# Output tiles kept in the weight buffers, stores behind the last load, and a new plan for a gated linear attention and spatial gating kernel

## The chip, the cores and the metric

The kernel runs on one core of one Trainium2 chip. The metric is the device time of one execution in microseconds, lower is better. The engines have short names: PE is the matrix engine, DVE the vector engine, ACT the scalar engine, POOL the GpSimd engine and SP the engine that issues nearly all transfers here. Each takes its instructions in the order in which the program gives them.

## The reference

Two layers follow each other. The first is a gated linear recurrence over 768 time steps for 4 batches and 8 heads of width 48; the second is a gated MLP that mixes over the sequence.

```python
# q, k, v, alpha: (B=4, H=8, S=768, D=48), float32
for t in range(S):
    state = alpha[:, :, t, :, None] * state + einsum('bhd,bhe->bhde', k[:, :, t], v[:, :, t])
    y[:, :, t] = einsum('bhd,bhde->bhe', q[:, :, t], state)
x = y.transpose(0, 2, 1, 3).reshape(B, S, H * D)          # (4, 768, 384)

h = maximum(x @ w_in, 0)                                   # w_in (384, 1024)
u, v = h[..., :512], h[..., 512:]
v_n = (v - mean(v)) / sqrt(var(v) + 1e-6)                  # over the last axis
v_s = einsum('ts,bsd->btd', w_spatial, v_n) + b_spatial[None, :, None]
out = (u * v_s) @ w_out                                    # (4, 768, 384), float32
```

## The kernel before, in words

The sequence is cut into 24 chunks of 128 rows, six for each of the four batches, numbered through. A chunk of the first layer loads four tiles, `ac` (alpha), `kc`, `qc` and `vc`, of 192 KB each. The first six chunks are loaded as three pairs of 384 KB. ACT takes the logarithm of `ac` into `la`. PE forms the running sum `cum` with a triangular matrix, and ACT takes exponentials of it: `binv`, the positive one in place, and `bc`, the decay of the whole chunk. POOL makes `kt` from `kc` and `binv`, DVE makes `qt` from `qc` and `cum`. PE transposes both into a PSUM bank (`pt`), and they are copied to `kqT`. PE then forms the scores, DVE masks them into `ptm` (two per chunk, called `m`), and PE adds the masked scores times the values `vb` and the queries times the carried state to `y`.

The state goes from chunk to chunk within a batch. PE forms its update `tp` (the operation `upd`), DVE adds it to the old state (`z`), `S` multiplies it by the decay (L334), and `sb` copies the two diagonal blocks to a bf16 tile `sbd` in two casts (L209). The next chunk's `y` reads `sbd`. `S` and `sb` may go to POOL or to DVE.

The output `y` is cast to `x_sb`, transposed on PE and copied to `xT`, which is the input of the second layer. There, for each batch, `v` (six tiles of 128x512) passes through ACT to `v_sb`. Its mean and variance come from DVE (`stats` and `mvs`) or, for the pairs of tiles that `ACT_STATS` names, from sums that ACT accumulates (L822 and L833) followed by three small DVE operations (`mv`). `rstd` is made on ACT and the normalised `vn` on DVE. `u` (eight groups of three matmuls) goes to `uT`. `s` (eight groups of six matmuls, `ps<-w_spT,vn`) is evacuated to `vsb` by DVE with the bias, and POOL multiplies it with `uT` to `gT`. The last `s` group takes its bias from a matmul and makes `gT` on DVE at once. `o` (six tiles per batch, four matmuls each) is evacuated by ACT and stored from SP.

The fp32 weights come in pieces of 768 KB into two buffers of the pool `raws` (`raw_w`) and are cast to bf16 tiles. The rows of `w_spatial` pass through three buffers `w_row` and are transposed into `w_spT`.

No order is written out by hand. Every operation is an `Op` with the engines that may run it, a planned duration, the operations that it waits for and a priority. `schedule` takes, again and again, the operation that can start first by these planned durations, and emits it; the instruction order on every queue comes from that. `PATIENCE` shifts the start that a kind of operation is compared by, `ENGINES` holds planned durations, `LD`, `LP`, `WT` and `ST` are those of transfers, and the argument `lat` is the time after which the result of an operation counts as there. `PIECES` places the weight loads among the others. While PE would be idle in the plan before 40 us, `schedule` puts matmuls of a tile `junk` in (L199), which compute nothing that is used and keep PE busy.

The output tiles go through a pool of four buffers `o_sb`, and their stores stand in SP's queue among the loads:

```python
def evac(eng, ps):
    hold["o"] = outp.tile([128, DM], FP32, name="o_sb")
    copy(eng, hold["o"], ps[:, 0:DM])
```

Of the kernel before, what the change touches and what calls it, by code (L numbers as in the profile page):

```python
# [9 lines left out]
FP32 = mybir.dt.float32  # L10
BF16 = mybir.dt.bfloat16
# [40 lines left out]
class Clock:  # L52
# [19 lines left out]
        return end  # L72


PATIENCE = {"ev": -0.3, "v": -0.1, "be": 0.2, "g": -0.3, "sb": -0.1, "bb": 0.3, "ln": 0.1, "z": -0.1, "S": 0.2, "o": -0.1, "cast": -0.2, "rs": 0.1}
ENGINES = {
    "kt": {"POOL": 0.87},
    "vb": {"POOL": 0.47},
    "S": {"POOL": 0.57, "DVE": 0.27},
    "sb": {"POOL": 0.79, "DVE": 0.36},  # L80
    "vn": {"DVE": 0.33},
    "xe": {"ACT": 0.38},
    "ev": {"DVE": 0.61, "ACT": 0.91},
    "u": {"ACT": 0.38, "DVE": 0.47},
    "o": {"ACT": 0.38},
}
PAIRS = (0, 1, 2)
ACT_STATS = ((0, 0), (3, 4), (2, 2), (3, 2))
PIECES = {
    "w_in": ((0, "vc", 0, 0.35), (0, "kc", 2, 0.15)),  # L90
    "w_sp": ((0, "vc", 4, 0.35), (0, "qc", 6, 0.25), (0, "qc", 6, 0.25)),
    "w_out": (0, "vc", 6, 0.35),
}


def schedule(ops, fill, warm_from, warm_to):

    free = {}
    clock = Clock()
    todo = list(ops)  # L100
    while todo:
        best = None
        for n, op in enumerate(todo):
            if any(d.end is None for d in op.deps):
                continue
            ready = max([d.end + d.lat for d in op.deps], default=0.0)
            waits = [slot.ring.free_at(k) for k, slot in enumerate(op.take)]
            if None in waits:
                continue
            ready = max([ready] + waits)  # L110
            for eng, dur in op.eng.items():
                start = max(ready, free.get(eng, 0.0))
                key = (round(start + (0.5 * dur if len(op.eng) > 1 else 0.0) + op.wait, 2),
                       ready if eng == "DMA" else op.prio)
                if best is None or key < best[0]:
                    best = (key, n, eng, start, dur)
        assert best is not None, "nothing can start"
        _, n, eng, start, dur = best
        op = todo.pop(n)
        if eng == "PE":  # L120
            if op.take and start < warm_to:
                t = max([free.get(eng, 0.0), warm_from] + [slot.ring.free_at(k) for k, slot in enumerate(op.take)])
                while True:
                    each = 0.00042 if clock.warm(t) else 0.00084
                    cols = min(192, int((start - t) / each) // 32 * 32)
                    if cols < 96:
                        break
                    fill.append(cols)
                    t = clock.run(t, 0.00042 * cols, cols)
            end = clock.run(start, dur, op.cols)  # L130
        else:
            end = start + dur
        for slot in op.take:
            slot.ring.taken.append(slot)
        free[eng] = end
        op.end = end
        op.emit(eng)
# [3 lines left out]
def kernel(  # L141
# [12 lines left out]
    nc = tc.nc  # L154

    B, H, S, D = q.shape
# [16 lines left out]
    IO = 3  # L173
    WK = 3
    NB, NKP = 3, 2
    LD, LP, WT, ST = 0.97, 1.46, 2.35, 0.8
    NRAW, NROW = 2, 3
    raws = ctx.enter_context(tc.tile_pool(name="raws", bufs=NRAW))
    io_pool = ctx.enter_context(tc.tile_pool(name="io", bufs=IO))
    work = ctx.enter_context(tc.tile_pool(name="work", bufs=WK))  # L180
# [13 lines left out]
    def bank(pool, shape, dtype, **kw):  # L194

        t = pool.tile(shape, dtype, **kw)
        flat = t if len(shape) == 2 else t.rearrange("p a b -> p (a b)")
        for cols in fill:
            nc.tensor.matmul(out=flat[:, 0:cols], lhsT=junk[:, 0:128], rhs=junk[:, 0:cols], start=True, stop=True)  # L199
        fill.clear()  # L200
        return t

# [15 lines left out]
    ut_ones = consts.tile([128, 128], BF16, name="ut_ones")  # L218
    ident = consts.tile([128, 128], BF16, name="ident")
    mask4 = consts.tile([128, 4, 128], BF16, name="mask4")  # L220
    junk = consts.tile([128, 192], BF16, name="junk")
    ones_row = consts.tile([1, 128], BF16, name="ones_row")
    ones_col = consts.tile([128, 1], BF16, name="ones_col")
    eps_tile = consts.tile([128, 1], FP32, name="eps_tile")
# [66 lines left out]
    def op(key, *args, **kw):  # L291

        users = kw.pop("use", ())
        o = Op(*args, **kw)
        for s in users:
            s.users.append(o)
        ops.append(o)
        made[key] = o
        o.wait = PATIENCE.get(key[0], 0.0)
        return o  # L300

    def got(*keys):
        return [made.get(x) for x in keys]
# [86 lines left out]
    def pair(j):  # L390
# [33 lines left out]
        for par in range(2):  # L424
# [42 lines left out]
                    out=ktp[:, par, :, :, 0:D].rearrange("p hp s d -> p (hp s) d"),  # L467
                    in0=st["kc"][:, :, par, :], in1=st[f"binv{par}"])

            op(("ktp", j, par), {"POOL": 0.87, "DVE": 0.47}, None, ktf, got(("einvp", j, par), ("kc", 2 * j)) + tr_users("k", jo), prio=P + 4)  # L470

            def qtf(_, par=par):
                nc.vector.tensor_mul(
# [116 lines left out]
    def first(i):  # L590
# [13 lines left out]

        j = i // 2
        jo = j - NKP
        dma(("ac", i), LD, load("ac", alpha), io_users("ln", j), P)
        dma(("kc", i), LD, load("kc", k), io_users("kt", j), P + 0.1)
        dma(("qc", i), LD, load("qc", q), io_users("qt", j), P + 0.2)
        dma(("vc", i), LD, load("vc", v), io_users("vb", j), P + 0.3)  # L610

        la, kt, qt = [x[j % NKP][:, i % 2].rearrange("p (hp s) d -> p hp s d", s=2) for x in (lap_bufs, ktp_bufs, qtp_bufs)]

# [196 lines left out]
    def second_v(b, tt):  # L810
# [33 lines left out]
        if on_act:  # L844
            def mv(_):
                d = bt[b]
                nc.vector.tensor_scalar_mul(out=d["mvs"][:, two, 0], in0=d["sums"][:, 0, two], scalar1=1.0 / DH)
                nc.vector.tensor_tensor(
                    out=d["mvs"][:, two, 1], in0=d["mvs"][:, two, 0], in1=d["mvs"][:, two, 0], op=ALU.mult)
                nc.vector.scalar_tensor_tensor(  # L850
                    out=d["mvs"][:, two, 1], in0=d["sums"][:, 1, two], scalar=1.0 / DH, in1=d["mvs"][:, two, 1],
                    op0=ALU.mult, op1=ALU.subtract)

            op(("mv", b, t0), "DVE", 0.4, mv, got(("bn", b, t0), ("bn", b, tt)), prio=6.0)

        def rs(_):
            d = bt[b]
# [38 lines left out]
    def second_s(b, dsl, th):  # L896
        last = b == B - 1 and dsl == NDS - 1 and th == 1
        mms = []
        if last:
            mms.append(mm(  # L900
                lambda ps: ps[:, 0:TH], lambda: ones_row, lambda: b_sp_sb[:, th * TH:(th + 1) * TH], True, False))
        for st in range(NT):
            mms.append(mm(
                lambda ps: ps[:, 0:TH], lambda st=st: bt[b]["vn"][:, st, dsl * 128:(dsl + 1) * 128],
                lambda st=st: w_spT[:, st, th * TH:(th + 1) * TH], st == 0 and not last, st == NT - 1))
        hold = {}
        cols = slice(th * TH, (th + 1) * TH)

        def evac(eng, ps):
            if last:  # L910
                nc.vector.tensor_tensor(
                    out=bt[b]["gT"][:, dsl, cols], in0=ps[:, 0:TH], in1=bt[b]["uT"][:, dsl, cols], op=ALU.mult)
            else:
                hold["vs"] = small.tile([128, TH], FP32, name="vsb", bufs=4)
                nc.vector.tensor_tensor(out=hold["vs"], in0=ps[:, 0:TH], in1=bsp_bc[:, th, :], op=ALU.add)  # L915

        Q = 1000.0 + 100 * b + 20 + th * NDS + dsl
        us = got(("u", b, dsl, th))
        pdeps = [[made[("vn", b, t)] for t in tt] for tt in ((0, 1, 2, 3), (4, 5))]
        us = us + got(*[("we", 3 * th + t) for t in range(3)])  # L920
        group(("s", b, dsl, th), mms, 0.165, [made[("v", b, t)] for t in range(NT)] + us,
              Q, evac, "DVE", 0.47,
              us + got(("be", th)) + [made.get(("o", b - 2, x)) for x in range(NT)], parts=2, pdeps=pdeps)
        if last:
            made[("g", b, dsl, th)] = made[("s", b, dsl, th)]
        else:
            def gm(eng):
                ENG[eng].tensor_tensor(  # L928
                    out=bt[b]["gT"][:, dsl, cols], in0=hold["vs"], in1=bt[b]["uT"][:, dsl, cols], op=ALU.mult)

            op(("g", b, dsl, th), {"POOL": 0.87} if b < B - 1 else {"POOL": 0.87, "DVE": 0.46}, None, gm, got(("s", b, dsl, th)), prio=Q)

    def second_o(b, tt):
        mms = [mm(
            lambda ps: ps[:, 0:DM], lambda dsl=dsl: bt[b]["gT"][:, dsl, tt * 128:(tt + 1) * 128],
            lambda dsl=dsl: w_out_sb[:, dsl, :], dsl == 0, dsl == NDS - 1) for dsl in range(NDS)]
        hold = {}

        def evac(eng, ps):
            hold["o"] = outp.tile([128, DM], FP32, name="o_sb")  # L940
            copy(eng, hold["o"], ps[:, 0:DM])

        Q = 1000.0 + 100 * b + 30 + tt
        group(("o", b, tt), mms, 0.165, [made[("g", b, x, tt // 3)] for x in range(NDS)] + made[("w_out",)], Q, evac,
              ENGINES["o"], None, [made.get(("st", b, tt - 4) if tt > 3 else ("st", b - 1, tt + 2))], parts=1)

        def store(_):
            nc.sync.dma_start(out=out[b, tt * 128:(tt + 1) * 128, :], in_=hold["o"])

        dma(("st", b, tt), ST, store, got(("o", b, tt)), -1.0, issue=0.8)  # L950
        made[("all", b)] = made[("st", b, tt)]


    op(("consts",), "POOL", 4.0, constants, prio=-10.0)
# [101 lines left out]
```

## Time and profile before

| | us |
|---|---|
| median of 11 runs | 158.89 (158.68 to 159.1) |
| the profiled execution | 158.97 |
| its span, first to last instruction | 157.2 |
| busy PE / DVE / ACT / POOL | 145.6 / 128.0 / 112.6 / 81.3 |
| DMA traffic | 28.62 MB, 182 GB/s mean |
| median from issue to landing: a 192 KB load / a store | 3.8 to 4.0 / 2.6 |

The busy times are those of one execution. Busy PE counts each matmul from start to end, and matmuls overlap each other. The slices of the page are 3.93 us wide. The granted clock of PE was 0.999 over the span. The rows of a group give count, total busy time and the mean of one in nanoseconds.

### The profile page before, as it was taken

How to read it: one execution, taken by the hardware profiler on the slowest of the kernel's cores; microseconds unless marked ns; L12 is line 12 of the kernel's file. 1: busy time of each engine (PE TensorE's matmuls, PEld its weight loads, DVE VectorE, ACT ScalarE, POOL GpSimd, SP SyncE). 2: the span in 40 equal slices, each digit the busy share in tenths (PEclk: the TensorE clock that was granted, in tenths of full speed). 3: DMA queues.
4: the chain of work that ended last, by engine and by line, in shares of the span. 5: the costliest groups of instructions: out<-in, count | busy, mean ns of one | idle time of the engine just before them, and what ended most of it. 6: DMA issues, size and time to landing. Idle time of an engine off the chain costs nothing.

```text
span 157.2 us, 4571 instructions
## 1 busy us (share of the span) xinstructions
PE 145.6 (93%) x1751; PEld 96.6 (61%) x1766; DVE 128.0 (81%) x279; ACT 112.6 (72%) x277; POOL 81.3 (52%) x131
## 2 busy tenths in 40 slices
PE   7999799999999989998899999799999999999970
PEld 6598467767656656666556666456666565656540
DVE  7769689697798999899899999996998997357620
ACT  3586595898998578879996678697878766770311
POOL 6737336656237664852377548475567364304320
PEclk9999999999999999999999999999999999999999
DMA  5999999998989799999999899999900004040224
GB/s 132 264 319 295 295 240 295 190 302 173 283 166 275 155 203 214 186 275 217 204 250 223 161 198 224 216 242 218 249 0 4 0 0 154 0 150 2 82 77 150
DMA packets 93015, 28.62 MB, mean 182 GB/s; under 512 B 87872, under 2 KB 91456, under 8 KB 92992
## 3 DMA queue, kind: packets, MB, share of 16 engines
q1 hardware_dynamic: 92960, 28.32, 76.8%
q8 instruction: 14, 0.23, 0.6%
q14 instruction: 9, 0.07, 0.1%
q0 software_dynamic: 32, 0.00, 0.0%
HBM read 23.60 MB, written 4.72 MB: 180 GB/s over the span
## 4 chain that ended last, share of the span: by engine, by line
PE 68%; DVE 17%; ACT 6%; issue 3%; DMA 2%; POOLq 1%; POOL 1%; ACTq 0%
PE ps L775 38%; PE pt L672 4%; DVE ptm L713 4%; PE pt L702 3%; DVE vsb L915 3%; DVE sbd L209 2%; PE ps L199 2%; PE y L363 2%; DMA ac<-in_alpha_dram 2%; PE y L730 2%; DVE stats L837 2%; PE y L573 2%; PE tp L688 2%; PE ps L430 2%; DVE ptm L557 2%
## 5 line engine op out<-in xcount | busy, mean ns | idle before, releaser
L928 POOL TENSOR_TENSOR gT<-vsb,uT 128x384 bf16<-128x384 f32 x28 | 26.1, 932 | 30.2 <-DVE vsb L915 29.7
L775 PE MATMUL ps<-w_spT,vn 128*128 128x384 bf16 x192 | 37.1, 326 | 0.0
L713 DVE TENSOR_TENSOR ptm<-pt,mask 128x512 bf16<-128x512 f32 x36 | 23.6, 679 | 1.1 <-PE pt L702 0.8
L645 POOL TENSOR_TENSOR kt<-kc,binv 128x384 bf16<-128x384 f32 x18 | 16.6, 926 | 14.1 <-ACT bc L640 7.8
L775 PEld LDWEIGHTS <-vn 128*128 128x128 bf16 x192 | 16.9, 97 | 9.4 <-issue 0.2
L915 DVE TENSOR_TENSOR vsb<-ps,bsp_bc 128x384 f32<-128x384 f32 x31 | 16.8, 548 | 4.3 <-PE ps L775 4.2
L207 ACT COPY o_sb<-ps 128x384 f32<-128x384 f32 x24 | 11.4, 480 | 12.1 <-PE ps L775 12.1
L775 PE MATMUL ps<-w_out_sb,gT 128*128 128x384 bf16 x96 | 17.6, 326 | 1.7 <-POOL gT L928 0.9
L775 PE MATMUL ps<-xT,w_in 128*128 128x384 bf16 x96 | 18.9, 326 | 0.0
L775 PE MATMUL ps<-w_in,xT 128*128 128x512 bf16 x57 | 16.6, 380 | 2.0 <-ACT xT L207 0.8
L334 POOL TENSOR_TENSOR state<-state,bc 128x192 f32<-128x192 f32 x15 | 7.7, 511 | 17.0 <-DVE state L329 8.5
L207 ACT CAST x_sb<-y 128x384 bf16<-128x384 f32 x24 | 11.5, 481 | 6.8 <-PE y L579 3.1
L775 PEld LDWEIGHTS <-gT 128*128 128x128 bf16 x96 | 9.1, 97 | 8.3 <-POOL gT L928 1.3
L837 DVE BATCH_NORM_STATS2 stats<-v_sb 128x6 f32<-128x512 bf16 x16 | 11.0, 687 | 3.3 <-ACT v_sb L213 3.3
L207 ACT COPY xT<-y 128x384 bf16<-128x384 bf16 x24 | 11.4, 480 | 2.7 <-PE y L363 2.4
L213 ACT ACTIVATE v_sb<-ps 128x512 bf16<-128x512 f32 x16 | 9.6, 600 | 4.3 <-PE ps L775 4.0
L199 PEld LDWEIGHTS <-junk 128*128 128x128 bf16 x117 | 10.8, 108 | 2.3 <-DVE junk L240 1.1
L209 DVE COPY kqT<-pt 128x1024 bf16<-128x1024 bf16 x15 | 10.3, 684 | 1.9 <-PE pt L672 1.5
L867 DVE TENSOR_SCALAR vn<-v_sb,mvs,rstd 128x512 bf16<-128x512 bf16 x24 | 11.6, 518 | 0.2
L213 ACT ACTIVATE uT<-ps 128x384 bf16<-128x384 f32 x23 | 10.7, 490 | 1.2 <-PE ps L775 1.2
L775 PEld LDWEIGHTS <-w_in 128*128 128x128 bf16 x96 | 8.3, 97 | 4.8
L775 PEld LDWEIGHTS <-xT 128*128 128x128 bf16 x72 | 6.1, 97 | 7.4 <-ACT xT L207 2.6
(127 smaller groups left out, 316.4 us busy)
## 6 DMA issues: line engine op xcount, KB each, us to landing
out_dram<-o_sb SPq DMA_DIRECT2D x24, 192.0 KB, 2.6
ac<-in_alpha_dram SPq DMA_DIRECT2D x18, 192.0 KB, 3.9
kc<-in_k_dram SPq DMA_DIRECT2D x18, 192.0 KB, 3.9
qc<-in_q_dram SPq DMA_DIRECT2D x18, 192.0 KB, 4.0
vc<-in_v_dram SPq DMA_DIRECT2D x18, 192.0 KB, 3.8
raw_w<-in_moe_w_spatial_dram SPq DMA_DIRECT2D x3, 768.0 KB, 5.8
raw_w<-in_moe_w_in_dram SPq DMA_DIRECT2D x2, 768.0 KB, 8.1
ac<-in_alpha_dram SPq DMA_DIRECT2D x3, 384.0 KB, 6.1
```

The costliest lines, as they stand in the source:

```text
L199: nc.tensor.matmul(out=flat[:, 0:cols], lhsT=junk[:, 0:128], rhs=junk[:, 0:cols], start=True, stop=True)
L207: nc.scalar.copy(out=out, in_=in_)
L209: ENG[eng].tensor_copy(out=out, in_=in_)
L213: nc.scalar.activation(out=out, in_=in_, func=AF.Relu)
L334: ENG[eng].tensor_tensor(out=st["state"], in0=st["state"], in1=st["bc"][:, :, None].to_broadcast([128, HP, D]), op=ALU.mult)
L645: ENG[eng].tensor_mul(out=kt[:, :, :, 0:D], in0=quad(st["kc"]), in1=st["binv"])
L713: nc.vector.tensor_tensor(out=st["ptm"][:, s], in0=st[f"pt{s}"], in1=mask4, op=ALU.mult)
L775: return lambda ps: nc.tensor.matmul(out=out(ps), lhsT=lhsT(), rhs=rhs(), start=start, stop=stop)
L837: nc.vector.bn_stats(out=stats, in_=d["v_sb"][:, tt, :])
L867: nc.vector.tensor_scalar(out=d["vn"][:, t, :], in0=d["v_sb"][:, t, :], scalar1=d["mvs"][:, t, 0:1], scalar2=d["rstd"][:, t:t + 1], op0=AL ...
L915: nc.vector.tensor_tensor(out=hold["vs"], in0=ps[:, 0:TH], in1=bsp_bc[:, th, :], op=ALU.add)
L928: ENG[eng].tensor_tensor(out=bt[b]["gT"][:, dsl, cols], in0=hold["vs"], in1=bt[b]["uT"][:, dsl, cols], op=ALU.mult)
```

## The change

Output tiles are counted through, n = 6 b + tt. Tiles 0 to 7 are evacuated to `raw_w` buffers, four to a buffer, which have the size of a weight piece; tiles 8 to 10 to `w_row` buffers; tiles 11 to 19 to `o_sb` as before; and tiles 20 to 23 to a `raw_w` buffer again. The stores of tiles 0 to 10 get a dependency on the issue of the last chunk's four loads. Tile 23 is evacuated in two halves, on ACT and on DVE. Four planned latencies of loads become 3.5 in place of 1.9. The planned durations are changed, each operation can have a shift of its own (`NUDGE`), `PATIENCE`, `ACT_STATS` (two pairs in place of four) and `PIECES` get other values, and a junk matmul may have 384 columns in place of 192. The shifts and costs change the order on every engine.

```diff
-PATIENCE = {"ev": -0.3, "v": -0.1, "be": 0.2, "g": -0.3, "sb": -0.1, "bb": 0.3, "ln": 0.1, "z": -0.1, "S": 0.2, "o": -0.1, "cast": -0.2, "rs": 0.1}
+PATIENCE = {"ev": -0.3, "kt": -0.2, "v": -0.1, "be": 0.2, "sb": 0.3, "bb": 0.2, "ln": 0.2, "z": -0.2, "we": -0.1, "S": 0.2, "cast": -0.1, "rs": 0.1, "trk": -0.1, "xs": -0.3, "xe": -0.2, "y": -0.2}
 ENGINES = {
-    "kt": {"POOL": 0.87},
-    "vb": {"POOL": 0.47},
-    "S": {"POOL": 0.57, "DVE": 0.27},
-    "sb": {"POOL": 0.79, "DVE": 0.36},
-    "vn": {"DVE": 0.33},
-    "xe": {"ACT": 0.38},
+    "kt": {"POOL": 0.9},
+    "vb": {"POOL": 0.48, "ACT": 0.42},
+    "S": {"POOL": 0.5, "DVE": 0.6},
+    "sb": {"POOL": 0.73, "DVE": 0.95},
+    "vn": {"DVE": 0.42},
+    "xe": {"ACT": 0.4},
...
+NUDGE = {
+    ("m", 9, 0): -0.15,
+    ("vn", 0, 4): -0.3,
+    ("qt", 22): -0.3,
...
+LATE = 3.5
-ACT_STATS = ((0, 0), (3, 4), (2, 2), (3, 2))
+ACT_STATS = ((2, 2), (0, 2))
 PIECES = {
-    "w_in": ((0, "vc", 0, 0.35), (0, "kc", 2, 0.15)),
+    "w_in": ((0, "vc", 1, 0.35), (0, "kc", 2, 0.15)),
...
-    "w_out": (0, "vc", 6, 0.35),
+    "w_out": (0, "qc", 7, 0.25),
...
-                    cols = min(192, int((start - t) / each) // 32 * 32)
+                    cols = min(384, int((start - t) / each) // 32 * 32)
...
-    LD, LP, WT, ST = 0.97, 1.46, 2.35, 0.8
-    NRAW, NROW = 2, 3
+    LD, LP, WT, ST = 1.03, 1.46, 2.35, 0.8
+    NRAW, NROW, KEEP = 2, 3, 11
...
-        o.wait = PATIENCE.get(key[0], 0.0)
+        o.wait = PATIENCE.get(key[0], 0.0) + NUDGE.get(key, 0.0)
...
-        dma(("ac", i), LD, load("ac", alpha), io_users("ln", j), P)
+        dma(("ac", i), LD, load("ac", alpha), io_users("ln", j), P, lat=LATE)
...
-            op(("mv", b, t0), "DVE", 0.4, mv, got(("bn", b, t0), ("bn", b, tt)), prio=6.0)
+            op(("mv", b, t0), "DVE", 0.9, mv, got(("bn", b, t0), ("bn", b, tt)), prio=6.0)
...
+    def out_tile(n):
+
+        if n < 8 or n >= B * NT - 4:
+            if n % 4 == 0:
+                kept["t"] = raws.tile([128, 4 * DM], FP32, name="raw_w")
+            return kept["t"][:, n % 4 * DM:(n % 4 + 1) * DM]
+        if n < KEEP:
+            return raws.tile([128, S], BF16, name="w_row", bufs=NROW).bitcast(FP32)
+        return outp.tile([128, DM], FP32, name="o_sb")
...
+        n = b * NT + tt
+        if n < 8:
+            free = [made[("cast", "w_out", x)] for x in range(NDS)] + [made[("cast", "w_sp", 2, x)] for x in range(2)]
+        elif n < KEEP:
+            free = got(("wt", n - 8 + 3))
+        elif n >= B * NT - 4:
+            free = got(*[("st", 0, x) for x in range(4)])
+        else:
+            free = got(("st", (n - 4) // NT, (n - 4) % NT)) if n >= KEEP + 4 else []
 
         def evac(eng, ps):
-            hold["o"] = outp.tile([128, DM], FP32, name="o_sb")
-            copy(eng, hold["o"], ps[:, 0:DM])
+            hold["o"] = out_tile(n)
+            if n < B * NT - 1:
+                copy(eng, hold["o"], ps[:, 0:DM])
+                return
+            half = DM // 2
+            copy("ACT", hold["o"][:, 0:half], ps[:, 0:half])
+            copy("DVE", hold["o"][:, half:DM], ps[:, half:DM])
...
         dma(("st", b, tt), ST, store, got(("o", b, tt)), -1.0, issue=0.8)
-        made[("all", b)] = made[("st", b, tt)]
+        if n < KEEP:
+            late.extend((made[("st", b, tt, "issue")], (x, N - 1, "issue")) for x in ("ac", "kc", "qc", "vc"))
+        made[("all", b)] = made[("o", b, tt)]
```

In the program that comes out of this, SP's queue holds all loads first and all 24 stores behind them; before, nine of the stores stood among the loads.

More of the change, by code (lines that the diff above doesn't have):

```diff
@@ L72, in run @@
         return end
-PATIENCE = {"ev": -0.3, "v": -0.1, "be": 0.2, "g": -0.3, "sb": -0.1, "bb": 0.3, "ln": 0.1, "z": -0.1, "S": 0.2, "o": -0.1, "cast": -0.2, "rs": 0.1}
+PATIENCE = {"ev": -0.3, "kt": -0.2, "v": -0.1, "be": 0.2, "sb": 0.3, "bb": 0.2, "ln": 0.2, "z": -0.2, "we": -0.1, "S": 0.2, "cast": -0.1, "rs": 0.1, "trk": -0.1, "xs": -0.3, "xe": -0.2, "y": -0.2}
 ENGINES = {
-    "kt": {"POOL": 0.87},
-    "vb": {"POOL": 0.47},
-    "S": {"POOL": 0.57, "DVE": 0.27},
-    "sb": {"POOL": 0.79, "DVE": 0.36},
-    "vn": {"DVE": 0.33},
-    "xe": {"ACT": 0.38},
-    "ev": {"DVE": 0.61, "ACT": 0.91},
-    "u": {"ACT": 0.38, "DVE": 0.47},
-    "o": {"ACT": 0.38},
+    "kt": {"POOL": 0.9},
[4 more added lines that the diff above has]
+    "xe": {"ACT": 0.4},
+    "ev": {"DVE": 0.61, "ACT": 0.91},
+    "u": {"ACT": 0.39, "DVE": 0.49},
+    "o": {"ACT": 0.4},
+}
+NUDGE = {
+    ("m", 9, 0): -0.15,
+    ("vn", 0, 4): -0.3,
+    ("qt", 22): -0.3,
+    ("upd", 2): 0.3,
+    ("v", 0, 5): 0.6,
+    ("vbp", 0, 0): -0.6,
+    ("z", 21): 1.5,
+    ("ebc", 0): 0.15,
+    ("ev", "q", 1, 1): 0.15,
+    ("z", 19): -1.5,
+    ("cast", "w_in", 0, 1): -0.15,
+    ("vb", 21): -0.15,
+    ("y", 19): -1.5,
+    ("kc", 0): 1,
+    ("o", 3, 2, "mm", 0): 0.3,
+    ("sc", 1, 0): -0.3,
+    ("tr", "k", 0, 1): -0.3,
+    ("qtp", 0, 0): -0.15,
+    ("y", 2): 0.15,
+    ("xs", 22): -0.3,
+    ("m", 20, 0): 0.6,
 }
 PAIRS = (0, 1, 2)
-ACT_STATS = ((0, 0), (3, 4), (2, 2), (3, 2))
+LATE = 3.5
+ACT_STATS = ((2, 2), (0, 2))
 PIECES = {
-    "w_in": ((0, "vc", 0, 0.35), (0, "kc", 2, 0.15)),
+    "w_in": ((0, "vc", 1, 0.35), (0, "kc", 2, 0.15)),
     "w_sp": ((0, "vc", 4, 0.35), (0, "qc", 6, 0.25), (0, "qc", 6, 0.25)),
-    "w_out": (0, "vc", 6, 0.35),
+    "w_out": (0, "qc", 7, 0.25),
 }
@@ L198, in bank @@
         for cols in fill:
-            nc.tensor.matmul(out=flat[:, 0:cols], lhsT=junk[:, 0:128], rhs=junk[:, 0:cols], start=True, stop=True)
+            for c in range(0, cols, flat.shape[1]):
+                n = min(cols - c, flat.shape[1])
+                nc.tensor.matmul(out=flat[:, 0:n], lhsT=junk[:, 0:128], rhs=junk[:, 0:n], start=True, stop=True)
         fill.clear()
@@ L220 @@
     mask4 = consts.tile([128, 4, 128], BF16, name="mask4")
-    junk = consts.tile([128, 192], BF16, name="junk")
+    junk = consts.tile([128, 384], BF16, name="junk")
     ones_row = consts.tile([1, 128], BF16, name="ones_row")
@@ L468, in ktf @@
                     in0=st["kc"][:, :, par, :], in1=st[f"binv{par}"])
-            op(("ktp", j, par), {"POOL": 0.87, "DVE": 0.47}, None, ktf, got(("einvp", j, par), ("kc", 2 * j)) + tr_users("k", jo), prio=P + 4)
+            op(("ktp", j, par), {"POOL": 0.9, "DVE": 0.6}, None, ktf, got(("einvp", j, par), ("kc", 2 * j)) + tr_users("k", jo), prio=P + 4)
             def qtf(_, par=par):
@@ L606, in first @@
         jo = j - NKP
-        dma(("ac", i), LD, load("ac", alpha), io_users("ln", j), P)
-        dma(("kc", i), LD, load("kc", k), io_users("kt", j), P + 0.1)
-        dma(("qc", i), LD, load("qc", q), io_users("qt", j), P + 0.2)
-        dma(("vc", i), LD, load("vc", v), io_users("vb", j), P + 0.3)
+        dma(("ac", i), LD, load("ac", alpha), io_users("ln", j), P, lat=LATE)
+        dma(("kc", i), LD, load("kc", k), io_users("kt", j), P + 0.1, lat=LATE)
+        dma(("qc", i), LD, load("qc", q), io_users("qt", j), P + 0.2, lat=LATE)
+        dma(("vc", i), LD, load("vc", v), io_users("vb", j), P + 0.3, lat=LATE)
         la, kt, qt = [x[j % NKP][:, i % 2].rearrange("p (hp s) d -> p hp s d", s=2) for x in (lap_bufs, ktp_bufs, qtp_bufs)]
@@ L929, in gm @@
                     out=bt[b]["gT"][:, dsl, cols], in0=hold["vs"], in1=bt[b]["uT"][:, dsl, cols], op=ALU.mult)
-            op(("g", b, dsl, th), {"POOL": 0.87} if b < B - 1 else {"POOL": 0.87, "DVE": 0.46}, None, gm, got(("s", b, dsl, th)), prio=Q)
+            op(("g", b, dsl, th), {"POOL": 0.9} if b < B - 1 else {"POOL": 0.9, "DVE": 0.69}, None, gm, got(("s", b, dsl, th)), prio=Q)
+    kept = {}
+    def out_tile(n):
[6 more added lines that the diff above has]
+        return outp.tile([128, DM], FP32, name="o_sb")
     def second_o(b, tt):
@@ L937, in second_o @@
         hold = {}
-        def evac(eng, ps):
-            hold["o"] = outp.tile([128, DM], FP32, name="o_sb")
-            copy(eng, hold["o"], ps[:, 0:DM])
+        n = b * NT + tt
[7 more added lines that the diff above has]
+            free = got(("st", (n - 4) // NT, (n - 4) % NT)) if n >= KEEP + 4 else []
+        def evac(eng, ps):
+            hold["o"] = out_tile(n)
[5 more added lines that the diff above has]
+            copy("DVE", hold["o"][:, half:DM], ps[:, half:DM])
         Q = 1000.0 + 100 * b + 30 + tt
         group(("o", b, tt), mms, 0.165, [made[("g", b, x, tt // 3)] for x in range(NDS)] + made[("w_out",)], Q, evac,
-              ENGINES["o"], None, [made.get(("st", b, tt - 4) if tt > 3 else ("st", b - 1, tt + 2))], parts=1)
+              ENGINES["o"], None, free, parts=1)
         def store(_):
```

## The prediction

> **What bounds the kernel now.** I read the page's busy shares and slices first, then the busy time by stage, then each load against its first use, then the end of the chain of waits. Page and stages (columns: PE, PEld, DVE, ACT, POOL busy us, then clock, DMA share, GB/s):
>
> ```profile
> PE 145.6 (93%) x1751; PEld 96.6 (61%) x1766; DVE 128.0 (81%) x279; ACT 112.6 (72%) x277; POOL 81.3 (52%) x131
> ...
> DVE  7769689697798999899899999996998997357620
> ...
> DMA  5999999998989799999999899999900004040224
> ```
> ```profile
> 52.00:76.00 24.00, 22.01 (x253) 13.88 (x255) 23.02 (x50) 19.81 (x49) 14.04 (x21) 1.00 1.01 212
> 76.00:104.00 28.00, 26.69 (x316) 17.28 (x318) 26.91 (x56) 22.08 (x60) 17.35 (x25) 1.00 1.00 213
> 104.00:128.00 24.00, 23.75 (x287) 15.45 (x289) 21.40 (x47) 18.97 (x52) 14.43 (x25) 1.00 0.42 97
> ```
>
> Until slice 29 (114 us) the DMA engines are full, and from 52 to 104 us DVE is 96% busy. PE looks full too, but its share counts pipelined matmuls: a 384-column one lasts 326 ns in the groups, while the chain below holds 71 in 11.98 us, 0.169 each. With start-to-start times instead, PE works about 42 of the 52 us from 75.9 to 127.9 (my estimate, 81%).
>
> DMA or DVE? Loads against their users:
>
> ```profile
> L602 SPq DMA_DIRECT2D ac<-in_alpha_dram x18: 433/746/3375, 21.6 to 106.1; - x18
> ...
> L615 ACT ACTIVATE la<-ac x18: 507/527/544, 29.8 to 116.7; 128x384 bf16<-128x384 f32 x18
> ```
>
> A load lands a median 3.9 us after its issue, so the last `ac` lay ready at 110.1 and was used at 116.7. Followed load by load, `ac` lands 1.8, 3.2 and 3.2 us ahead of its `la` for chunks 11, 12 and 13 and 6.6 us ahead for chunk 23; the last `kc` waits 14.9 us. So DMA still sets the pace until about chunk 13 (its `qt` starts at 75.9), and then DVE does, with the loads running away from it. In the last stage (from 134.1, the last `y`) PE sets it:
>
> ```profile
> 138.12 11.98 PE ps L775 x71
> 150.09 0.02 issue
> 150.11 0.57 DVE vsb L915
> ...
> 151.78 1.81 PE ps L775 x10
> ```
>
> **What the Trainium skill says.** "Perfetto Trace Analysis", Identifying the Most-Contended Engine: occupancy is a fair measure for VectorE, not for matmuls; the 0.169 against 0.326 agrees. "SBUF — State Buffer", Who interferes with whom: a VectorE copy or cast between SBUF tensors can take the port pair shared with GpSimd, and the later of the two blocks wholly. The `sbd` casts agree: on DVE they range from 240 to 956 ns (mean 423), and `state` on DVE (two SBUF inputs) from 348 to 1107.
>
> ```profile
> L209 DVE CAST sbd<-state x22: 240/257/956, 12.4 to 124.6; 64x192 bf16<-64x192 f32 x22
> ...
> L209 POOL CAST sbd<-state x18: 336/345/674, 26.7 to 117.2; 64x192 bf16<-64x192 f32 x18
> ```
>
> **The change part by part.** Counts are from the two programs' order, durations from this trace; the sum is made against the profiled execution (158.97, span 157.2, 1.77 around it, 0.08 above the median).
>
> 1. *Stores.* Nine stores are issued ahead of the last load now (66.1 to 102.4 us); tiles 9 and 10 already come behind it. Afterwards none is ahead. 192 KB at the 213 GB/s of that stage is 0.92 us, so the last load lands up to 9 x 0.92 = 8.3 us sooner, at about 104.6 in place of 112.9. By itself that is worth nothing after chunk 13, as the loads are early anyway; before chunk 13 only the three stores at 66 us could matter. It matters as room: without it a faster DVE would catch up with the loads. On SP eleven stores then follow the last load, 0.4 to 0.8 us of issue each, so until about 112; no load is behind them, and the next `o_sb` slot that waits for a store belongs to tile 15 (batch 2), evacuated later. Tiles 0 to 7 wait for the casts of `w_out` (done by 55.0), which their own matmuls need anyway, tiles 8 to 10 for `wt` (done by 48.9), tiles 20 to 23 for stores 0 to 3, landed some 35 us earlier. All zero.
>
> 2. *DVE.* Gone: 22 `sbd` casts x 0.423 = 9.3; 2 `state` x 0.52 = 1.0; 2 `kqT` x 0.684 = 1.4; two rows of `mv` (0.66 each) = 1.3. Added: 4 `stats` and `mvs` x 0.87 = 3.5; half an output tile, 0.35; the bias copy and a `w_spT` cancel. Net **-9.2 us**. Of the durations queued ahead of chunk 13's `qt` it takes 72.9 to 67.1; between the `qt` of 13 and 23, 52.6 to 48.0.
>
> 3. *ACT and POOL.* ACT loses four `sq` and the accumulating `v_sb` reads and gains two `kqT`, five value casts: -1.2 net. POOL gains 22 `sbd` x 0.366 = 8.1, 2 `state`, loses 5 value casts: +7.8. POOL is 62% busy from 76 to 104, so the work fits, but in a FIFO.
>
> 4. *Junk matmuls.* 117 of at most 192 columns become 71 of at most 384: 21.8 to 22.8 thousand columns, +0.4 us of PE, before 40 us, where PE waits for loads. A junk of 384 can hold a real matmul back by 0.17 us more. The trace has no such piece; I bound the effect at -1 to +1 us and take 0.
>
> 5. *Order of loads.* The same to chunk 17 but for one swap; later `vc` goes ahead of `kc`/`qc`. They land 7 to 15 us early: zero.
>
> 6. *Tail.* Behind the last `y` stand 106 matmuls of 384 columns, afterwards 97: 9 x 0.169 = -1.5. At the end PE idles 0.89 us (150.9 to 151.8) for `gT`; the new order puts two output tiles (4 x 0.169 = 0.68 us each) into and behind the last `s` group: -0.9. Against it, only about 6.2 us of PE work now lie between the last `y` and the first `s` that needs its `vn`, about as long as the chain `x_sb`, `xT`, `v_sb`, `stats`, `rstd`, `vn` (some 5.4 of durations and hand-offs): 0 to +0.7, I take +0.3. The halved last evacuation is tile 23, and tile 20 is evacuated behind it: zero.
>
> *Sum by stage.* To chunk 13: DVE gives 5.8, but the loads leave at most 3.2: I take half of that, -1.6. From 13 to 23: DVE gives -4.6; PE would rise from 81% to 89% and ACT with it, in FIFOs, so I take half, -2.3. Tail: -2.1. Together -6.0: span 151.2, time **153.0**.
>
> **The rivals.**
> - *Absorbed.* DVE gets emptier but PE and ACT wait in order for other things; only the tail and a little more comes: -0.5 to -3, about 157. For it: ACT is 79% busy from 76 to 104 and the order was rewritten everywhere. Against: those waits are short now (the longest group of ACT, 12.1 us for `o_sb`, lies mostly behind 104 us).
> - *DVE all the way.* All 10.4 us ahead of the last `qt` come through, plus the tail: -10 to -12, about 148. Against: the loads forbid most of the first 5.8.
> - *Slower: the recurrence on POOL.* Every `sbd` now queues on POOL, behind a `gT` or `kt` of 0.93 us, and `y` of the next chunk waits for it on PE, with all of PE's queue behind. POOL waits are long: `gT` waited 29.7 us in total for `vsb`, once 8.1. If each of 20 chunks loses 0.5 us, 10 us go: -6 + 10, about 163. It decides from 0.3 us a chunk. Against: POOL did nine of the twenty already, and its cast (2 x 0.37) is shorter than DVE's blocked one (2 x 0.42).
> - That the change does not do what it says: in part true, nine stores move, not eleven; counted above.
>
> **How the numbers follow.** Likeliest 0.59 (150 to 156); absorbed 0.21 (156 to 158.6); all of DVE 0.11 (146 to 150); slower 0.09. Leaving out about one in ten at each end, unknowns of junk and contention included: 148.8 to 158.6. A measurement here tells 0.2% (0.3 us) from no change. Faster 0.89: the first three, less 0.02 of the absorbed; same 0.03; slower 0.08.
>
> **What would show it.** Right: no store before the last load, which is issued at 100 to 103; DVE near 119 us in all and under 93% from 76 to 104; `la` of chunk 23 near 110 to 113; the last `y` at 129 to 131 and no PE gap near the end. Wrong: PE gaps released by POOL `sbd` (slower); DVE still at 96% with `vn` casts longer than their mean 518 ns, from contention with the busier POOL (absorbed); a last `y` before 126 (all of DVE).

## The result and the profile after

The changed kernel takes 154.94 us (median; 154.67 to 155.14) against 158.81 us: the ratio is 0.9751, with a 95% interval of 0.9738 to 0.9763. It is faster by 3.9 us, as forecast in direction and inside the range, but 1.9 us short of the 153.0 forecast. Some executions of one kernel take 1 to 3 us longer than its median, and the ratios leave out those over 1.5% above its fastest. The profiled execution has a span of 153.2 us, 4.0 less than before.

The page of the changed kernel: busy us, the slices of DVE and of DMA, and the stages as in the prediction (PE, PEld, DVE, ACT, POOL, clock, DMA share, GB/s).

```profile
PE 144.9 (95%) x1702; PEld 91.9 (60%) x1720; DVE 119.8 (78%) x256; ACT 112.0 (73%) x270; POOL 87.4 (57%) x152
...
DVE  7766599494879999897989999487979897756820
...
DMA  4999999999999996997999989999960013400053
```
```profile
52.00:76.00 24.00, 23.41 (x267) 15.14 (x268) 21.94 (x47) 19.92 (x51) 16.71 (x29) 1.00 0.95 186
76.00:104.00 28.00, 27.35 (x323) 17.50 (x324) 23.91 (x51) 23.19 (x61) 18.27 (x29) 1.00 1.01 199
104.00:128.00 24.00, 23.61 (x283) 15.33 (x286) 21.39 (x45) 18.91 (x45) 17.21 (x28) 1.00 0.47 147
```

DVE has lost 8.2 us and POOL has gained 6.1. From 76 to 104 us DVE is 85% busy in place of 96%. What PE leaves idle from 52 to 104 us fell from 52 - 22.01 - 26.69 = 3.30 us to 1.24 us. These are gaps in which no matmul is in flight at all; as a matmul counts as busy for 326 ns and takes 0.169 us in a row, shorter waits between matmuls do not show in them.

The loads of `ac` and their users, again from the view by tile:

```profile
L628 SPq DMA_DIRECT2D ac<-in_alpha_dram x18: 542/736/2603, 21.7 to 99.3; - x18
L641 ACT ACTIVATE la<-ac x18: 507/527/556, 33.7 to 113.8; 128x384 bf16<-128x384 f32 x18
```

The last `ac` is issued 6.8 us sooner than before, its user starts only 2.9 us sooner: the loads ran further away from the work. The first single-chunk `la` starts at 33.7 in place of 29.8, later than before.

The end of the chain of waits, and the last copies of ACT and DVE for tile 23 from the timeline (start, duration, instruction, idle time before it and what ended that):

```profile
134.09 14.63 PE ps L801 x87
148.72 0.02 issue
148.74 0.48 ACT raw_w L233
```
```profile
148.09 0.32 ACT L233 COPY raw_w<-ps 128x192 f32<-128x192 f32 x1 [0.17 <-PE ps L801]
148.44 0.36 DVE L235 COPY raw_w<-ps 128x192 f32<-128x192 f32 x1 [2.32 <-ACT raw_w L233]
```

PE runs to its end with no gap for `gT`. But the DVE half of tile 23 started only when ACT's half had ended, at 148.41; the two do not overlap.

### The profile page after: what moved, and what is told of

Same layout as the page of the kernel before. It is cut to its first block, busy times and chain, and to the rows that moved or that the text cites. A ratio compares the mean times of both kernels' runs of the same rounds, so it can differ in the third digit from the quotient of the medians.

```text
span 153.2 us, 4470 instructions
## 1 busy us (share of the span) xinstructions
PE 144.9 (95%) x1702; PEld 91.9 (60%) x1720; DVE 119.8 (78%) x256; ACT 112.0 (73%) x270; POOL 87.4 (57%) x152
## 4 chain that ended last, share of the span: by engine, by line
PE 87%; ACT 4%; issue 2%; DVE 2%; POOL 1%
PE ps L801 47%; PE pt L698 6%; PE ps L225 5%; PE pt L728 3%; PE y L389 3%; PE cum L647 2%; PE y L756 2%; PE ps L456 2%; PE tp L714 2%; PE y L599 2%; PE y L750 2%; PE ps L521 2%; PE ps L811 2%; PE y L225 2%; PE pt L572 1%
## 5 line engine op out<-in xcount | busy, mean ns | idle before, releaser
L801 PE MATMUL ps<-w_spT,vn 128*128 128x384 bf16 x192 | 36.1, 326 | 0.0
L801 PE MATMUL ps<-w_out_sb,gT 128*128 128x384 bf16 x96 | 18.2, 326 | 0.0
L863 DVE BATCH_NORM_STATS2 stats<-v_sb 128x6 f32<-128x512 bf16 x20 | 13.7, 684 | 5.0 <-ACT v_sb L239 4.8
L801 PE MATMUL ps<-w_in,xT 128*128 128x512 bf16 x54 | 15.3, 380 | 1.4 <-issue 0.4
L239 ACT ACTIVATE v_sb<-ps 128x512 bf16<-128x512 f32 x20 | 11.9, 597 | 6.0 <-PE ps L801 5.1
L360 POOL TENSOR_TENSOR state<-state,bc 128x192 f32<-128x192 f32 x17 | 8.7, 512 | 11.4 <-DVE state L353 7.3
L235 POOL CAST sbd<-state 64x192 bf16<-64x192 f32 x40 | 13.8, 344 | 2.3 <-DVE state L360 0.5
L233 ACT COPY o_sb<-ps 128x384 f32<-128x384 f32 x9 | 4.3, 482 | 9.9 <-PE ps L801 9.9
L681 DVE TENSOR_TENSOR qt<-qc,cum 128x384 bf16<-128x384 f32 x18 | 9.8, 547 | 0.8 <-ACT cum L676 0.6
L659 ACT ACTIVATE binv<-cum 128x384 bf16<-128x384 f32 x18 | 8.7, 492 | 2.2 <-POOL sbd L235 0.7
```

The costliest lines, as they stand in the source:

```text
L233: nc.scalar.copy(out=out, in_=in_)
L235: ENG[eng].tensor_copy(out=out, in_=in_)
L239: nc.scalar.activation(out=out, in_=in_, func=AF.Relu)
L681: nc.vector.tensor_mul(out=qt[:, :, :, 0:D], in0=quad(st["qc"]), in1=st["cv"])
L801: return lambda ps: nc.tensor.matmul(out=out(ps), lhsT=lhsT(), rhs=rhs(), start=start, stop=stop)
L863: nc.vector.bn_stats(out=stats, in_=d["v_sb"][:, tt, :])
```

## The experiments

To undo or add one part without a new plan, the order was frozen: `schedule` first makes its whole list of operations and engines, a function `edit` changes that list, and only then the instructions are emitted. Each time is a median; the ratios are to the kernel before, measured on the same chip beside it. A difference from the changed kernel is one of medians; taken from the two ratios it comes out up to 0.4 us larger or smaller. In the edits, `...` marks lines left out.

**The casts alone, in the kernel before.**

```diff
-    return plan
+    return [(op, "POOL" if op.key[0] == "sb" else eng, junks) for op, eng, junks in plan]
```

> The kernel before, its order frozen, with one part of the change: the eleven chunk states whose two casts to sbd ran on DVE have them on POOL, at the same places of the emission order. Theory 'DVE sets the pace from about chunk 13': DVE loses some 9 us of busy time and the time falls by 1.5 to 3.5 us, to 155.3 to 157.3, with the last qt starting 1.5 to 3 us sooner than 127.8. Rival 'the recurrence on POOL': the casts queue behind gT and kt, y comes late, and the time rises by 1 us or more. Rival 'only a new order brings it': within 0.5 us of 158.8.

157.72 us, ratio 0.9916 (0.989 to 0.9942): 1.3 us faster, a little less than the 1.5 that the theory asked for. DVE fell from 128.0 to 120.0 us, POOL rose from 81.3 to 88.2. The last `qt` starts at 126.9, 0.9 sooner, less than the 1.5 expected; 0.8 of that lies behind chunk 13, whose `qt` starts at 75.7 in place of 75.9. The recurrence on POOL does not bite, and DVE relief is worth something without any new order, but only a third of the whole gain.

**The stores alone, in the kernel before.** The nine tiles go to the weight buffers as well.

```diff
+    held = [x for x in plan if x[0].key[0] == "st" and x[0].key[-1] == "issue" and 6 * x[0].key[1] + x[0].key[2] < 9]
+    rest = [x for x in plan if x not in held]
+    at = max(n for n, x in enumerate(rest) if x[0].key[-1] == "issue" and x[0].key[0] in ("ac", "kc", "qc", "vc"))
+    return rest[:at + 1] + held + rest[at + 1:]
...
```

> The kernel before, its order frozen, with the other part alone: tiles 0 to 8 are evacuated to the weight buffers and their nine stores stand behind the last load on SP. Theory 'the loads are early anyway': the last load lands 4 to 6 us sooner than 112.9 and the time stays within 0.4 us of 158.8. Rival 'DMA sets the pace': the time falls by 1.5 us or more.

159.21 us, ratio 1.0026 (1.0012 to 1.004): 0.4 us slower, if anything. The last load landed at 112.8, no sooner than the 112.9 before, so the expected 4 to 6 us did not come either. In the other runs with stores among the loads it landed between 112.9 and 116.8, in those of the changed order with stores behind between 107.9 and 110.8; the time does not follow it.

**Both in the kernel before.** The two edits above together.

> The kernel before with both edits, casts on POOL and stores behind the last load, in the frozen order. Theory 'the stores are only room': the same as with the casts alone, within 0.5 us. Rival 'a faster DVE runs into the loads': at least 1 us faster than with the casts alone.

157.42 us, ratio 0.9913 (0.9892 to 0.9934), the same as with the casts alone. In this order no room was wanted.

**Tile 23 undivided, in the changed kernel.**

```diff
-            if n < B * NT - 1:
-                copy(eng, hold["o"], ps[:, 0:DM])
-                return
-            half = DM // 2
-            copy("ACT", hold["o"][:, 0:half], ps[:, 0:half])
-            copy("DVE", hold["o"][:, half:DM], ps[:, half:DM])
+            copy(eng, hold["o"], ps[:, 0:DM])
```

> The changed kernel in its own frozen order, tile 23 evacuated whole by ACT. In the changed kernel the DVE half waits for the ACT half, so the store of tile 23 leaves at 148.82 and that of tile 20 at 149.25, and the last lands 2.8 us later in place of 1.9. Theory 'the halves bunch the last two stores': the store of tile 23 leaves 0.2 us sooner, the last lands 0.2 to 0.8 us sooner, time 154.1 to 154.8. Rival 'the late landing has another cause, such as the instruction transfer that is in flight then': within 0.15 us of 154.94.

153.90 us, ratio 0.9678 (0.9662 to 0.9695): 1.0 us faster than the changed kernel, more than either theory allowed, and the fastest version that computes the whole result. The last two stores are issued at 148.43 and 149.08 and land 1.9 us after issue; in the changed kernel they are issued at 148.82 and 149.25 and the last lands at 152.09, 2.8 us after issue.

**The casts put back, in the changed kernel.** The same eleven states, to DVE.

```diff
+    back = (0, 1, 2, 7, 8, 10, 12, 14, 15, 16, 22)
+    return [(op, "DVE" if op.key[0] == "sb" and op.key[1] in back else eng, junks) for op, eng, junks in plan]
```

> The changed kernel, its order frozen, with the casts to sbd of the same eleven states back on DVE, at the same places of the emission order. Theory 'DVE relief is worth the 1.3 us that the casts alone brought to the kernel before': 1 to 2.5 us slower than the 154.94 of the changed kernel. Rival 'in the new order DVE has room': within 0.5 us of it. Rival 'the casts on POOL cost the recurrence something': faster than it.

158.27 us, ratio 0.9956 (0.9926 to 0.9987): 3.3 us slower than the changed kernel, more than any theory had. The profile is of an execution that took 160.57 us, so its later stages are not compared. Up to 29.9 us its clock was full, though, and at 28.4 us PE is already 2.3 us behind the changed kernel. There, first in the changed kernel and then in this one, DVE and POOL do this:

```profile
23.58 0.91 DVE L893 TENSOR_SCALAR vn<-v_sb,mvs,rstd 128x512 bf16<-128x512 bf16 x2
24.42 1.27 DVE L583 TENSOR_TENSOR ptm<-pt,mask 128x512 bf16<-128x512 f32 x2
24.57 1.88 POOL L492 TENSOR_TENSOR kt<-kc,binvp 128x384 bf16<-128x384 f32 x2 [0.22 <-ACT bc L487]
```
```profile
24.16 0.85 DVE L246 CAST sbd<-state 64x192 bf16<-64x192 f32 x2
25.05 2.12 DVE L905 TENSOR_SCALAR vn<-v_sb,mvs,rstd 128x512 bf16<-128x512 bf16 x2
27.09 1.27 DVE L595 TENSOR_TENSOR ptm<-pt,mask 128x512 bf16<-128x512 f32 x2
25.15 1.88 POOL L504 TENSOR_TENSOR kt<-kc,binvp 128x384 bf16<-128x384 f32 x2 [0.25 <-ACT bc L499]
```

In the changed kernel the two `vn` end before POOL begins its two `kt`. With a pair of casts ahead of them they run beside the `kt` and take 2.12 us in place of 0.91, and `ptm`, for which PE waits, comes 2.7 us later. So the casts on DVE are worth 1.3 us in the old order and 3.3 in the one that was planned without them, but the 3.3 is not a price of DVE work alone: a good part of it is lost ahead of chunk 6, at a place where the order had no room for them.

**The stores put back, in the changed kernel.** `ready` holds the stores whose tile has been evacuated.

```diff
...
+        if key[-1] == "issue" and key[0] in ("ac", "kc", "qc", "vc"):
+            out += ready
+            ready = []
...
```

> The changed kernel, its order frozen, with the nine stores of tiles 0 to 8 put back among the loads, each ahead of the first load issue that follows its evacuation in the emission order; the tiles stay in the weight buffers. Theory 'the loads are early anyway': the last load lands 4 to 5 us later than 107.9, and the time stays within 0.4 us of 154.94. Rival 'the new order uses the room': 1 us slower or more.

155.05 us, ratio 0.9731 (0.9686 to 0.9776), within 0.1 us of the changed kernel, although the last load lands at 116.8 in place of 107.9. With the run above from the other side, the move of the stores is worth nothing measurable.

**Less work for DVE, in the changed kernel.** The variance is taken over 64 of 512 columns.

```diff
-            nc.vector.bn_stats(out=stats, in_=d["v_sb"][:, tt, :])
+            nc.vector.bn_stats(out=stats, in_=d["v_sb"][:, tt, 0:64])
```

> The changed kernel with the twenty stats of DVE over 64 columns in place of 512, so that the variance is taken over an eighth of each row; order and waits as they are. Some 20 x 0.45 = 9 us of DVE work go. Theory 'DVE still limits the middle': 2 us or more faster than 154.94. Rival 'PE in its order limits it now': at most 1 us faster.

154.64 us, ratio 0.9708 (0.9669 to 0.9746): 0.3 us faster (0.7 by the ratios) for 9.2 us less of DVE:

```profile
PE 144.7 (95%) x1702; PEld 91.9 (60%) x1720; DVE 110.6 (72%) x256; ACT 111.9 (73%) x270; POOL 87.4 (57%) x152
```

**Less work for PE, in the changed kernel.** In `v` and in `u` of batches 0 to 2 the third of three products is left out and the second matmul stops the sum, so this kernel does not compute the whole result.

```diff
...
+        if b < B - 1:
+            mms[2] = lambda ps: None
...
```

> The changed kernel in its frozen order with the third of three accumulating matmuls left out of every v and u group of batches 0 to 2, so that a third of their inputs is not summed: 18 x 0.216 + 24 x 0.162 = 7.8 us less of PE work, nearly all ahead of the last y. Theory 'PE limits the middle of the changed kernel': the last y comes 2.5 us or more before 131.7, and the time falls by as much. Rival 'chains through several engines in their fixed order limit it': at most 1 us faster, as with the shorter stats (0.3 us).

151.53 us, ratio 0.9527 (0.9498 to 0.9555): 3.4 us faster for 7.8 us less of PE work by the count above, with the last `y` at 128.1 in place of 131.7. Of DVE's relief 3 to 7% came through, of PE's about 44%. The page, and the stages from 52 to 104 us:

```profile
PE 138.7 (93%) x1661; PEld 87.4 (58%) x1678; DVE 119.0 (80%) x256; ACT 110.9 (74%) x270; POOL 87.8 (59%) x152
```
```profile
52.00:76.00 24.00, 22.89 (x278) 14.59 (x281) 22.59 (x50) 20.64 (x53) 16.64 (x31) 1.00 0.98 193
76.00:104.00 28.00, 26.23 (x316) 16.79 (x318) 24.50 (x53) 24.20 (x63) 19.12 (x31) 1.00 0.97 191
```

In the changed kernel PE, in the order that it is given, holds the middle more than DVE does. That it alone sets the pace is not shown: a `v` or `u` of two matmuls is also ready sooner for ACT, and more than half of the relief became idle time, which from 52 to 104 us rises from 1.24 to 2.88 us.

**The tail's order alone, in the kernel before.** Tile 20 goes behind the last `s` group.

```diff
+    o = [x for x in plan if x[0].key[:3] == ("o", 3, 2)]
+    rest = [x for x in plan if x not in o]
+    at = max(n for n, x in enumerate(rest) if x[0].key[0] == "s" and x[1] == "PE")
+    rest[at + 1:at + 1] = o
...
```

> The kernel before, its order frozen, with one output tile of the last batch (tile 20, four matmuls) moved behind the last s group on PE, as the new order has it. Theory 'PE idles for gT at the end': the idle time of 0.89 us ahead of the last matmuls shrinks to about 0.25 and the time falls by 0.4 to 0.7 us. Rival 'POOL's gT arrives as late as before and only the place of the gap moves': within 0.2 us of 158.9.

158.32 us, ratio 0.9949 (0.9927 to 0.9971): 0.65 us faster, as much as the gap shrinks, from 0.89 to 0.24. The timelines of PE, first of the kernel before, then of this one, show the gap for `gT` (in brackets) filled by four matmuls more:

```profile
150.40 0.49 PE L775 MATMUL ps<-w_out_sb,gT 128*128 128x384 bf16 x2
151.78 1.80 PE L775 MATMUL ps<-w_out_sb,gT 128*128 128x384 bf16 x10 [0.89 <-POOL gT L928]
```
```profile
149.53 1.14 PE L795 MATMUL ps<-w_out_sb,gT 128*128 128x384 bf16 x6
150.92 1.80 PE L795 MATMUL ps<-w_out_sb,gT 128*128 128x384 bf16 x10 [0.24 <-POOL gT L948]
```

**The last tile in two buffers and two stores.** Tile 23 whole; tile 20, evacuated last, in two halves.

```diff
...
+                hold["l"] = outp.tile([128, DM], FP32, name="o_sb")[:, 0:half]
+                hold["r"] = outp.tile([128, DM], FP32, name="o_sb")[:, 0:half]
+                copy("DVE", hold["r"], ps[:, half:DM])
+                copy("ACT", hold["l"], ps[:, 0:half])
...
```

> The changed kernel in its frozen order with tile 23 whole on ACT, and the tile that really comes last, tile 20, in two halves on DVE and ACT, each in a buffer of its own with a store of its own (the left one issued from ACT's queue). Theory 'the DVE half waited because both halves lay in one buffer': the halves run side by side, the last evacuation ends 0.1 us sooner and half the bytes are left to store, 0.1 to 0.5 us below the 153.9 of the undivided version. Rival 'reads of one PSUM tile wait for each other': the second half starts when the first has ended, 153.9 or more.

154.88 us, ratio 0.9727 (0.971 to 0.9743): 1.0 us slower than the undivided version. A buffer of its own for each half did not help:

```profile
148.69 0.36 DVE L245 COPY o_sb<-ps 128x192 f32<-128x192 f32 x1 [2.62 <-PE ps L812]
149.08 0.32 ACT L243 COPY o_sb<-ps 128x192 f32<-128x192 f32 x1 [0.56 <-DVE o_sb L245]
```

In the program ACT's copy waits for DVE's semaphore, and the PSUM tile is all that the two share. Split, the evacuation takes 0.36 + 0.32 = 0.68 us in place of 0.48.

**No single shifts.** The changed kernel with an empty `NUDGE`, planned anew.

```diff
-NUDGE = {
...
-}
+NUDGE = {}
```

> The changed kernel with an empty NUDGE, so planned anew. Theory 'planned durations and the casts on POOL bring most of the gain': 0 to 2 us slower than 154.94. Rival 'the single shifts bring it': 2 to 5 us slower.

154.99 us, ratio 0.9767 (0.9712 to 0.9823): no difference is seen, but one of the four executions took 156.59, and the interval leaves room for 0.9 us either way. The last `y` is 1.6 us sooner (130.1), with 105 in place of 97 matmuls of 384 columns behind it, and PE ends 0.45 us later. Here the halved tile is the last; its store lands 1.8 us after issue, so the late landing of the changed kernel is not in this profile and makes up for that.

**Planned durations alone, in the kernel before**, planned anew.

```diff
...
-    "S": {"POOL": 0.57, "DVE": 0.27},
-    "sb": {"POOL": 0.79, "DVE": 0.36},
...
+    "S": {"POOL": 0.5, "DVE": 0.6},
+    "sb": {"POOL": 0.73, "DVE": 0.95},
...
```

> The kernel before with the planned durations of the changed kernel alone (ENGINES, kt of the pairs, mv, g), planned anew; stores, PATIENCE, ACT_STATS, PIECES and latencies as before. The plan now gives one of twenty pairs of casts to DVE. Theory 'planned durations near the measured ones bring most of the gain ahead of the tail': 1.5 to 3.5 us faster than before. Rival 'they only move the casts': as with the casts alone, 0.5 to 1.5 us faster, or slower still.

158.94 us, ratio 0.9993 (0.9974 to 1.0011): nothing, which neither theory expected. Yet PE's idle time from 52 to 104 us is 1.22 us here, as small as in the changed kernel:

```profile
52.00:76.00 24.00, 23.53 (x259) 15.18 (x262) 20.03 (x42) 20.56 (x53) 16.89 (x26) 1.00 0.98 203
76.00:104.00 28.00, 27.25 (x328) 17.87 (x331) 25.36 (x52) 24.20 (x62) 18.81 (x31) 1.00 0.94 196
```

The last `y` is 1.8 us sooner than before (132.3), but 115 matmuls of 384 columns stand behind it in place of 106, and the old form of the tail keeps its gap for `gT`:

```profile
151.57 1.80 PE L775 MATMUL ps<-w_out_sb,gT 128*128 128x384 bf16 x10 [0.96 <-POOL gT L928]
```

## Why the prediction was right, and where it was not

The direction held, and in the main so did the mechanism of the middle and of the tail; that of the first stage did not. Stage by stage, in the profiled spans:

| stage | predicted | measured |
|---|---|---|
| to chunk 13's `qt` (75.9 before, 75.0 after) | -1.6 | -0.9 |
| from there to chunk 23's `qt` (52.0 before, 49.9 after) | -2.3 | -2.1 |
| from there to PE's end (25.7 before, 23.8 after) | -2.1 | -1.9 |
| from PE's end to the end of the span (3.6 before, 4.5 after) | 0 | +0.9 |
| sum | -6.0 | -4.0 |

Of the signs named in advance, no store stands before the last load, DVE is at 119.8 us and at 85%, and PE has no gap near its end. Three came about a microsecond late: the last load is issued at 104.2 in place of 100 to 103, `la` of chunk 23 starts at 113.8 in place of 110 to 113, and the last `y` at 131.7 in place of 129 to 131.

1. *Stores.* The value, zero, was right, shown from both sides. The working was not: nine stores behind the loads were to bring the last load 8.3 us forward. In the changed kernel it came 4.9 us sooner, in the kernel before not at all. The price of 0.92 us a store assumed the loads' rate; where the stores go out alone, the slice of the changed kernel shows 387 GB/s, which makes 0.5 us. That no load would be missed held; that the room mattered did not in either order.

2. *DVE and POOL.* -8.2 and +6.1 us stand against -9.2 and +7.8. The casts on POOL took 344 ns, not 366. `vn` grew from a mean of 518 to 537 ns, 0.5 us in all, which agrees with the contention for the shared port that the Trainium skill ("SBUF — State Buffer", Who interferes with whom) leads one to expect. The traces show it: over all fourteen profiles the 120 `vn` with no POOL instruction beside them took 398 to 414 ns, and each of those that took 1.0 us and more, 31 in all, ran beside a `kt` or `gT` on POOL. With a mean of 518 ns, 113 above the usual 405 of these, that came to some 24 x 0.113 = 2.7 us of DVE before the change already (my estimate); the change added 0.5.

3. *The middle.* That half of DVE's relief would come through was a choice without a working behind it, so that it came out at -2.1 is in part luck. The reason given, that PE and the others in their fixed order would take the rest, agrees with the shorter stats and the shorter sums: less work for PE still brings time, less for DVE hardly any. The casts alone explain 1.3 us; what else the middle gained came with the new order, and which part of that order brought it is not shown.

4. *The first stage.* Here the failed step is "the loads leave at most 3.2: I take half". The loads were not what held: `ac` of chunk 13 lay ready for 5.5 us in the changed kernel. The new order starts chunks 6 and 7 later, and DVE works less in these stages, 9.4 of the 14 us from 26 to 40 in place of 11.1. The kernel with planned durations alone starts `la` of chunk 6 at 29.9, as before, the one without single shifts at 33.5, as the changed one, so neither of these makes it late; the longer planned latency of the loads, the priorities and the places of the weight loads were not tried apart. It is only shown that the loads did not hold it.

5. *The tail.* The count of matmuls and the filled gap held on PE: -1.9, and 0.65 of that is shown alone. From the last `y` to PE's end it is -2.5 us, against -2.4 for these two terms; the other 0.6 was lost between the last `qt` and the last `y`, not to a gap behind it, for which the prediction took 0.3. The failed step is "The halved last evacuation is tile 23, and tile 20 is evacuated behind it: zero". It costs 1.0 us, and with it undivided the kernel reaches 153.90. The halves run one after the other, so the store of tile 23 leaves 0.39 us later and the last 0.17 later; 0.16 of each is that PE itself ends later in that profile. Nearly all of the microsecond is the last landing. Read packet by packet, a transfer of 8 KB of instructions starts at 150.50, between the packets of the last store. By 150.80 all but seven of these have started; the seven follow one at a time, the last at 151.57. The same meeting, with 2.8 to 2.9 us from issue to landing, is in the profiles with the stores put back, with the shorter stats and with the shorter sums; with the last tile in two buffers the instruction transfer (at 150.37) also falls among the last packets, and the half store lands after 2.4 us. In the undivided version the instruction transfer comes at 152.72, behind all stores. Bunching is probably not the cause of the late landing: with the casts put back, in one execution, the two last stores leave 0.43 us apart as well, the instruction transfer comes 4 us ahead of them, and the last lands after 2.0 us. That it is the transfer which delays the packets is inferred from these coincidences; it could not be moved by itself. So how far the halving itself costs the 1.0 us, and how far it only shifts the program against that transfer, is open.

6. *Junk matmuls* of up to 384 columns were not tried apart. That one could hold a real matmul back by 0.17 us more is a slip: 0.16 is the whole of it, against 0.08 for the 192 columns of before. The rival that the recurrence suffers on POOL is refuted by both runs with the casts; of the rival in which all of DVE's relief comes through, the shorter stats show why it did not.

What stays open is about 3 us between the undivided version (-5.0) and the parts that were shown alone in the kernel before (casts -1.3, tail order -0.65). Planned durations alone bring nothing, and for the single shifts nothing is seen; the other priorities, latencies and the choice of `stats` engine were not separated.

## What to carry to other kernels

Two engines may both look nearly full; take the relief of one at full value only until the next in the chain has no gaps left, and find out which that is by making each lighter in turn, as the shorter stats (0.3 us for 9.2) and the shorter sums (3.4 us for 7.8) did. PE's gaps alone do not tell the time: planned durations alone closed them as far as the whole change did and brought nothing, because the work moved behind the last `y`. Ask of every evacuation cut in two whether the halves may overlap and what the last store meets. Moving transfers away from loads that already lie ready 7 to 15 us early buys nothing. An edit put into an order that was not made for it can cost or bring much more or less than its busy time (3.3 against 1.3 us), as it also shifts which instructions run side by side.

## What the runs showed of the hardware that was not expected

An instruction transfer of 8 KB that fell among the packets of the last 192 KB store went with a landing 2.8 to 2.9 us after issue in four profiles; where none fell among the last two stores it was 1.8 to 2.0 us, and where it fell among those of the store before, in the two kernels with stores moved in the old order, 2.1. That is about 0.9 us at the very end of the kernel. A `vn` on DVE took 398 to 414 ns with no POOL instruction beside it and up to 1168 ns beside a `kt` or `gT`; at one place of the order, two of them took 0.91 us just ahead of two `kt` and 2.12 us beside them. And with the same order of loads, the last load landed at 112.9, 114.9 and 116.0 us in the profiles of three kernels (before, casts alone, tail's order alone), while their times did not follow.
